# The capacity's cast moved ahead of the last rows, and six gates a step sooner, in a routed expert kernel

## The chip, the cores and the metric

One core of a Trainium2 chip. The metric is the device time of one execution in microseconds (us); three runs of the kernel before are at hand, and one profiled execution.

## The reference

3072 tokens (4 batches of 768) pass through three stages in a row:

```python
for t in range(S):                      # attention: B=4, H=8, S=768, D=40
    y[:, :, t] = einsum('bhd,bhde->bhe', rt, state)
    Sa = einsum('bhde,bhe->bhd', state, at)
    state = state * wt - einsum('bhd,bhe->bhde', Sa, bt) + einsum('bhd,bhe->bhde', vt, kt)
...
logits = x @ w_gate                     # 8 experts, x is 3072 x 320
expert_idx = argmax(logits)             # one expert for each token
gate_w = softmax(logits)[expert_idx]
...
h = maximum(disp[e] @ w1[e], 0)         # 320 -> 1024, up to `capacity` tokens an expert
out[i] = gate_w[i] * (h @ w2[e])        # 1024 -> 320
...
h = x @ w_in                            # 320 -> 2048
out = where(h > 0, h, exp(min(h, 0)) - 1) @ w_out
```

`capacity` is an input (768 here): a token that comes to an expert after its capacity is full gets zeros.

## The kernel before, in words

The program runs in one launch: `attention()` up to about 437 us of the span, then `ffn()`. Every engine works off its instructions in the order in which the program gives them out; nothing is reordered afterwards, so "ahead of" and "behind" in this text mean that order on one engine.

**Attention.** Its steps stand in a table written out by hand (ORDER, from L33 on). Near its end the table has `b22.1 D21 F H22 q23.1`: `b` is `route()`, which picks each token's expert and ends with the sum ACC (L547); `D` scatters a group's rows to the experts' table `disp` in HBM; `F` is `first()` (L597), which makes two index rows on GpSimd (POOL) and issues the loads of the first rows; `q` and what follows (Qs, L487; y, L509; XT, L513; x, L519) is the last group's way through attention. Rows of the first expert that are already in `disp` are loaded from there, transposed (L668), and those of the last two groups of tokens are added by matmuls with a one-hot matrix (L593). The sum stands in the PSUM tiles `pt`.

**Experts.** `experts()` (L1191) makes eight blocks, one for each expert, of 448 slots. `run()` (L1157) goes through their steps. A block has eight steps f = 0 to 7, one for each 128 columns of F. All numbers are split into two parts, a high part (H, XH) and the rest (L, XL), and every product takes the matmuls high by high, low by high and high by low. In step f it gives out, in this order:

- `s1(f)` (L969): eight matmuls of the first layer into a PSUM tile `ph`;
- `s2(f-3)` (L1034 to L1042): eight matmuls of the second layer, into three `po` tiles;
- `act`, here `relu` (L1097), for step f-1: H on ACT (L1099), L on DVE (L1100);
- one piece of the next expert's `load()` (in `rows()`, L1082): it issues the load of X (L1086, on SP), then come two halves of `soft()` (L1068), the softmax that gives the gate g. The first half is a reduction and a subtraction on DVE (L1073, L1074) and an exponential on ACT (L1075); the second half is three DVE instructions (L1077 to L1079). Then four scalings of X by g on ACT (L1093);
- in the last three of the pieces, `prep()` (L944): four transposes on PE into a PSUM tile `pt` (L934), XH on ACT (L953), XL on DVE (L954);
- `extra()`: weight splits, of which the high part is a cast on ACT (L776) and the low part four subtractions on POOL (L781), the fetches of later weights on SP, and pieces of a table conversion on DVE (L859 to L871).

The PSUM tiles of `s1` and the `pt` tiles take turns in four buffers, so a new one waits for the last reader of the tile four before it. A block's result is read out of the `po` tiles while the next block runs (L1047 to L1050). The fifth step of each block (f = 4) gives out the first transposes for the next expert behind its matmuls. Expert 0 has its rows ready in PSUM at the start, unscaled; its gate comes late (`late_gate()`, L1277) and is multiplied in at the end.

Ahead of the first block stand a weight split of four pieces, 16 subtractions on POOL, and `marks()` (L1259), which turns the capacity, an integer of two 32-bit words, to a float: a cast (L1262) and three small instructions (L1263 to L1265), all on DVE. Its users come much later: `gates()` (L1116) and `counts()` (L1372 to L1375).

After the experts come six blocks of the second feed-forward layer, with `elu` in place of `relu`, up to the end. They are not touched.

Of the kernel before, what the change touches and what calls it, by code (L numbers as in the profile page):

```python
# [8 lines left out]
F32 = mybir.dt.float32  # L9
F32R = mybir.dt.float32r  # L10
I32 = mybir.dt.int32
U32 = mybir.dt.uint32
AF = mybir.ActivationFunctionType
ALU = mybir.AluOpType
# [8 lines left out]
SL = 448  # L23
# [52 lines left out]
def attention(tc, nc, e_in, v_tok, d_in, wg, disp, xt, cst, ring, early, early_w, cv, cap, after):  # L76
# [29 lines left out]
    Ws = sh[3][:, 2688:2816].rearrange("p (h t) -> p h t", t=16)  # L106
# [488 lines left out]
    cols, turned = [slice(128 * k, 128 * k + (128, 128, 65)[k]) for k in range(3)], []  # L595

    def first():  # L597
        nc.gpsimd.iota(cst["row"], pattern=[[1, 112]], base=SL, channel_multiplier=0, allow_small_or_imprecise_dtypes=True)
        nc.gpsimd.iota(cst["off"], pattern=[[-112, 4]], base=0, channel_multiplier=0, allow_small_or_imprecise_dtypes=True)
        first_rows(nc, cst, disp)  # L600
# [13 lines left out]
    def warm(n):  # L614
        w = early_w.B[0]
        p = bank("warm")
        for _ in range(n):
            nc.tensor.matmul(p, w[:, 0:128], w[:, 0:512], start=True, stop=True)
    steps = dict(sz=set_z, se=set_e, sa=set_a, sd=set_d, sv=set_v, st=set_t, sr=set_r, ss=set_s, sx=set_x, sw=set_w, sc=set_c, lw=load_w,
                 e=load_e, E=lambda u: load_e(u, eng=nc.scalar), v=load_v, d=load_d, p=pre, a=pre_act, c=scores, m=am_evac, k=kb_tr, l=lm_load, i=solve, o=x_store,  # L620
# [62 lines left out]
def consts(p):  # L683

    c = {}
    c["ident"] = p.tile([128, 128], F32, name="ident")
    c["mask"] = p.tile([128, 64], F32, name="mask")
    for nm in ("ones", "tri"):
        c[nm] = p.tile([128, 128], BF, name=nm)
    c["desc"] = p.tile([128, 8], F32, name="desc")  # L690
    c["ebase"] = p.tile([128, 8], F32, name="ebase")
    c["lg"] = p.tile([128, 24, 9], F32, name="LG")
    c["oh"] = p.tile([128, 2, 8, 12], BF, name="OH")
    c["slot"] = p.tile([128, 24], I32, name="SLOT")
    c["acc"] = p.tile([128, 2, 8], BF, name="ACC")
    c["cap"] = p.tile([128, 2], I32, name="CAP")
    c["x"] = p.tile([128, 2048], F32, name="X0")
    c["xo"] = c["x"][:, 1536:1536 + RW]
    c["row"] = c["x"][:, 1536 + RW:1648 + RW]
    c["off"] = c["x"][:, 1648 + RW:1652 + RW]  # L700
    return c
# [185 lines left out]
def ffn(tc, nc, cst, disp, xt, w1, w2, w32, out, ring, W0, cv, ps, turned):  # L887
# [3 lines left out]
    ap = ctx.enter_context(tc.tile_pool(name="fa", bufs=2))  # L891
# [187 lines left out]
        nc.vector.reciprocal(g, g)  # L1079
        return g  # L1080

    def rows(src, gate=True):  # L1082

        def load(s, now):
            s.X = s.XF[:, 0:4 * RW].rearrange("p (i d) -> p i d", i=4)
            nc.sync.dma_start(out=s.X[0:112], in_=src)  # L1086
            yield
            if not gate:
                return
            yield  # L1090
            g = yield from soft(s)
            for i in range(4):
                nc.scalar.mul(s.X[0:112, i, 0:D], s.X[0:112, i, 0:D], g[:, i:i + 1])  # L1093
            yield
        return load

    def relu(p, H, L):  # L1097
# [18 lines left out]
    def gates():  # L1116

        OH = cst["oh"]
        T = lambda nm, sh, dt=F32: gp.tile(sh, dt, tag="g" + nm, name=nm, bufs=1)
        for nm in ("blk", "tmo", "l1"):  # L1120
            cst[nm] = T(nm, [128, 128], BF)
        set_gates(nc, cst)
        m = T("m", [128, 2, 8, 12])
        nc.vector.memset(m, 1.0)
        nc.vector.memset(m[:, :, :, 0:1], 0.0)
        ic = T("ic", [128, 2, 8, 12], BF)
        nc.vector.tensor_tensor_scan(
            out=ic.rearrange("p b e c -> p (b e c)"), data0=m.rearrange("p b e c -> p (b e c)"),
            data1=OH.rearrange("p b e c -> p (b e c)"), initial=0.0, op0=ALU.mult, op1=ALU.add)
        S = T("S", [128, 2, 8], BF)  # L1130
        nc.vector.tensor_copy(S, ic[:, :, :, 11])
        p = ps.tile([128, 512], F32, tag="ph", name="pg")
        p1 = p[:, 0:192]
        nc.tensor.matmul(p1, cst["tmo"], OH.rearrange("p b e c -> p (b e c)"), start=True, stop=False)
        nc.tensor.matmul(p1, cst["blk"], ic.rearrange("p b e c -> p (b e c)"), start=False, stop=True)
        nc.tensor.matmul(p[:, 192:208], cst["l1"], S.rearrange("p b e -> p (b e)"), start=True, stop=False)
        nc.tensor.matmul(p[:, 200:208], cst["ones"], S[:, 0], start=False, stop=True)
        b = T("b", [128, 2, 8])
        nc.vector.tensor_copy(b.rearrange("p b e -> p (b e)"), p[:, 192:208])
        t = T("t", [128, 2, 8, 12])  # L1140
        nc.vector.tensor_tensor(t, p1.rearrange("p (b e c) -> p b e c", b=2, e=8),
                                b.unsqueeze(3).to_broadcast([128, 2, 8, 12]), op=ALU.add)
        nc.vector.scalar_tensor_tensor(out=t, in0=t, scalar=over["cap"], in1=OH, op0=ALU.is_lt, op1=ALU.mult)
        kp = T("kp", [128, 24])
        nc.vector.tensor_reduce(kp.rearrange("p (c b) -> p b c", b=2), t.rearrange("p b e c -> p b c e"), axis=AX.X, op=ALU.add)
        eb0 = T("eb0", [128, 8])
        nc.vector.tensor_scalar(eb0, cst["ebase"], float(-SL), None, op0=ALU.add)
        nc.vector.tensor_tensor(t, OH, eb0.unsqueeze(1).unsqueeze(3).to_broadcast([128, 2, 8, 12]), op=ALU.mult)
        eb = T("eb", [128, 24])
        nc.vector.tensor_reduce(eb.rearrange("p (c b) -> p b c", b=2), t.rearrange("p b e c -> p b c e"), axis=AX.X, op=ALU.add)  # L1150
        pos, epos = T("pos", [128, 24]), T("epos", [128, 24])
        nc.vector.tensor_tensor(pos, cst["slot"], eb, op=ALU.subtract)
        nc.vector.tensor_scalar(pos, pos, float(-SL), None, op0=ALU.add)
        nc.vector.scalar_tensor_tensor(out=epos, in0=eb, scalar=1.0 / 8, in1=pos, op0=ALU.mult, op1=ALU.add)
        return kp, pos, epos
# [29 lines left out]
    dv = disp.rearrange("(e r i p) d -> e r p i d", e=8, i=4, p=112)  # L1185
# [5 lines left out]
    def experts(r, dyn=False, more=None):  # L1191
# [3 lines left out]
        bl = []  # L1195
        for e in range(8):
# [8 lines left out]
            else:  # L1205
                def store(Y, e=e):
# [1 line left out]
                    nc.sync.dma_start(out=xt[0:256, c].rearrange("(k p) n -> p k n", p=128), in_=Y[:, 0:2])  # L1208
                    nc.sync.dma_start(out=xt[256:D, c], in_=Y[0:64, 2])
                    nc.sync.dma_start(out=xt[D:D + 1, c], in_=Y[64:65, 2])  # L1210
                bl.append(Turned(Ws[e], rows(dv[e, 1], e > 0), relu, store, P=112))
        if dyn:
            for _ in ahead(Ws[0]):
                pass
# [43 lines left out]

    def marks():  # L1259

        cw, cf = cst["cap"], ap.tile([128, 4], F32, name="cf", bufs=1)
        nc.vector.tensor_copy(cf[:, 0:2], cw)  # L1262
        nc.vector.tensor_scalar(cf[:, 2:3], cf[:, 0:1], 0.0, 4294967296.0, op0=ALU.is_lt, op1=ALU.mult)  # L1263
        nc.vector.scalar_tensor_tensor(out=cf[:, 3:4], in0=cf[:, 1:2], scalar=4294967296.0, in1=cf[:, 2:3], op0=ALU.mult, op1=ALU.add)
        nc.vector.tensor_tensor(cf[:, 3:4], cf[:, 3:4], cf[:, 0:1], op=ALU.add)  # L1265
        over["cap"] = cf[:, 3:4]
        one = over["one"] = ap.tile([128, 8], F32, name="one", bufs=1)
        nc.gpsimd.memset(one, 1.0)
        start = over["start"] = ap.tile([128, 6], F32, name="begin", bufs=1)
# [86 lines left out]
    over = {}  # L1356

    def counts():
# [12 lines left out]
        rg = ap.tile([128, 8], F32, name="rg", bufs=1)  # L1371
        nc.vector.tensor_reduce(rn[:, 0:1], cnt, axis=AX.X, op=ALU.max)  # L1372
        nc.vector.tensor_scalar(rn[:, 1:2], rn[:, 0:1], float(SL // 8), None, op0=ALU.add)
        nc.vector.tensor_scalar(rn[:, 2:3], over["cap"], float(SL), None, op0=ALU.min)
        nc.vector.tensor_tensor(rn[:, 2:3], rn[:, 0:1], rn[:, 2:3], op=ALU.is_gt)  # L1375
        yield
        nc.vector.tensor_scalar(rg, cst["ebase"], 1.0 / 8, rn[:, 1:2], op0=ALU.mult, op1=ALU.is_lt)
# [128 lines left out]
```

## Time and profile before

| | us |
|---|---|
| three runs: median (lowest, highest) | 1044.39 (1041.87, 1047.43) |
| the profiled execution, its own time | 1040.54 |
| its span | 1038.7 |
| PE busy | 950.6 (92%) |
| DVE busy | 738.3 (71%) |
| POOL busy | 617.1 (59%) |
| ACT busy | 516.6 (50%) |
| mean granted clock of TensorE | 0.952 of full speed |

All times in the rows are microseconds from the span's start. A row of the timeline has a start, how long a run of like instructions lasts, the engine, the line, what it writes and reads, and how many they are; in brackets how long its engine was idle ahead of it, and what the profile takes for the releaser. Idle time and its releaser are inferred, and where a wait has several causes the last one by the profile is named. PE is TensorE, PEld its weight load, SPq the queue that issues transfers. The profiled execution's 1040.54 us is its span and what lies around it.

### The profile page before, as it was taken

The numbers are of one execution on the slowest core, as the hardware profiler recorded it, in microseconds if no ns is written. First come the engines' busy times: TensorE is split into PE (matmuls) and PEld (weight loads), VectorE is DVE, ScalarE is ACT, GpSimd is POOL, SyncE is SP. The second block draws the span as 40 slices with busy tenths as digits, with TensorE's granted clock in tenths as the row PEclk, the third lists the DMA queues.
The fourth block names the chain that finished last, engine by engine and source line by source line (L and its number), as shares of the span: only waits on it lengthen the run. The fifth ranks groups of instructions, "written<-read, shape, count | busy, mean of one in ns | idle before, by whom it ended". The sixth has DMA issues, their size and how long they took to land.

```text
span 1038.7 us, 25351 instructions
## 1 busy us (share of the span) xinstructions
PE 950.6 (92%) x9994; PEld 860.9 (83%) x9994; DVE 738.3 (71%) x1291; ACT 516.6 (50%) x1013; POOL 617.1 (59%) x929
## 2 busy tenths in 40 slices
PE   4758989989899999789999999999999999999993
PEld 4758878888789888678889888888899888899993
DVE  8846848788675687658778877576766777677760
ACT  3636635666454434245544555565555555554550
POOL 4766979489898833467768787953333333333332
PEclk9967889999899999989999999999999999999997
DMA  6758875666565774646776866501010000100000
GB/s 161 174 159 173 182 162 120 144 139 145 127 120 119 171 195 99 170 141 203 214 236 201 250 186 217 187 23 26 27 27 26 11 28 13 27 26 1 26 2 28
DMA packets 181448, 121.69 MB, mean 117 GB/s; under 512 B 106256, under 2 KB 167336, under 8 KB 179688
## 3 DMA queue, kind: packets, MB, share of 16 engines
q1 hardware_dynamic: 175652, 99.63, 38.0%
q10 hardware_dynamic: 2500, 9.21, 3.4%
q0 software_dynamic: 3168, 11.14, 3.0%
q8 instruction: 81, 1.33, 0.5%
q14 instruction: 47, 0.39, 0.1%
HBM read 86.89 MB, written 33.05 MB: 115 GB/s over the span
## 4 chain that ended last, share of the span: by engine, by line
PE 54%; DVE 17%; DMA 16%; issue 5%; ACT 3%; POOL 3%; SPq 0%; ACTq 0%; DVEq 0%; POOLq 0%
PE ph L969 20%; DMA ring<-in_e_in_dram 5%; PE po L995 5%; PE po L996 5%; PE po L997 5%; DMA w<-E 4%; PE q L482 2%; PE sc L234 2%; DVE L L1100 1%; DVE ring L200 1%; PE x L519 1%; DVE E L860 1%; PE ut L426 1%; PE y L509 1%; DMA dab<-AB 1%
## 5 line engine op out<-in xcount | busy, mean ns | idle before, releaser
L781 POOL TENSOR_TENSOR ring<-ring,ring 128x64 fp32r<-128x64 f32 (+2 forms) x320 | 204.7, 675 | 72.4 <-ACT ring L776 72.4
L1114 POOL TENSOR_TENSOR L<-E,H 128x512 fp32r<-128x512 f32 x66 | 91.6, 1388 | 169.2 <-ACT H L1113 152.5
L969 PE MATMUL ph<-XH,ring 128*128 128x512 f32 (+1 forms) x640 | 169.9, 387 | 0.8 <-ACT XH L953 0.8
L1107 ACT ACTIVATE E<-N 128x512 f32<-128x512 f32 x96 | 60.7, 632 | 152.8 <-DVE N L1106 78.9
L310 POOL TENSOR_TENSOR X<-X,ring 128x60 f32<-128x60 f32 (+19 forms) x170 | 120.4, 708 | 13.3
L969 PEld LDWEIGHTS ph<-XH,ring 128*128 128x128 f32 x640 | 115.7, 190 | 14.9 <-ACT XH L953 1.4
L997 PE MATMUL po<-ring,L 128*128 128x320 f32 x384 | 119.4, 311 | 1.6 <-POOL L L1114 1.6
L995 PE MATMUL po<-ring,H 128*128 128x320 f32 x384 | 119.4, 311 | 0.2 <-ACT H L1113 0.2
L996 PE MATMUL po<-ring,H 128*128 128x320 f32 x384 | 119.2, 310 | 0.0
L969 PE MATMUL ph<-XL,ring 128*128 128x512 f32 (+1 forms) x320 | 97.9, 387 | 7.5 <-DVE XL L954 7.5
L969 PE MATMUL ph<-XS,ring 128*128 128x512 f32 (+1 forms) x320 | 96.9, 384 | 0.0
L1111 DVE SCALAR_TENSOR_TENSOR M<-E,M 128x512 f32<-128x512 f32 x96 | 78.0, 812 | 16.1 <-ACT M L1108 16.1
L1106 DVE TENSOR_SCALAR N<-ph 128x512 f32<-128x512 f32 x96 | 65.8, 685 | 27.7 <-PE ph L969 27.4
L308 POOL TENSOR_TENSOR ring<-X,ring 128x60 f32<-128x60 f32 (+19 forms) x108 | 65.0, 602 | 34.4 <-DMA ring<-dab 26.3
L995 PEld LDWEIGHTS po<-ring,H 128*128 128x128 f32 x384 | 72.8, 190 | 5.2 <-ACT H L1113 0.5
L996 PEld LDWEIGHTS po<-ring,H 128*128 128x128 f32 x384 | 72.7, 189 | 4.0
L969 PEld LDWEIGHTS ph<-XL,ring 128*128 128x128 f32 x320 | 60.7, 190 | 18.4 <-DVE XL L954 8.2
L997 PEld LDWEIGHTS po<-ring,L 128*128 128x128 f32 x384 | 72.7, 189 | 2.1 <-POOL L L1114 2.1
L1112 DVE SCALAR_TENSOR_TENSOR E<-ph,M 128x512 f32<-128x512 f32 x96 | 66.4, 692 | 8.1 <-DVE M L1111 0.5
L969 PEld LDWEIGHTS ph<-XS,ring 128*128 128x128 f32 x320 | 60.3, 189 | 11.2 <-DVE XS L954 0.4
L1100 DVE SCALAR_TENSOR_TENSOR L<-ph,H 128x448 fp32r<-128x448 f32 x64 | 39.4, 616 | 41.3 <-ACT H L1099 41.2
L1113 ACT CAST H<-E 128x512 fp32r<-128x512 f32 x96 | 59.0, 614 | 13.5 <-DVE E L1112 10.4
(261 smaller groups left out, 2176.5 us busy)
## 6 DMA issues: line engine op xcount, KB each, us to landing
ring<-in_w_dram SPq DMA_DIRECT2D x16, 640.0 KB
ring<-in_w_dram SPq DMA_DIRECT2D x32, 256.0 KB
dab<-AB SPq DMA_DIRECT2D x24, 256.0 KB
ring<-in_e_in_dram ACTq DMA_DIRECT2D x18, 321.6 KB
ring<-w SPq DMA_DIRECT2D x4, 1408.0 KB
disp<-ring SPq DMA_DIRECT2D x8, 575.8 KB
S<-in_w_out_dram SPq DMA_DIRECT2D x13, 320.0 KB
ring<-in_w_dram SPq DMA_DIRECT2D x32, 128.0 KB
```

Of the source, the lines that this page charges most:

```text
L308: nc.gpsimd.tensor_tensor(tv, X[:, 0:n, s:s + 1].to_broadcast([128, n, m]), N[:, s:s + 1, s + 1:e].to_broadcast([128, n, m]), op=ALU.mult)
L310: nc.gpsimd.tensor_tensor(X[:, 0:n, s + 1:e], X[:, 0:n, s + 1:e], tv, op=ALU.subtract)
L781: s.nc.gpsimd.tensor_tensor(B[:, to], r[:, q], B[:, q].bitcast(F32), op=ALU.subtract)
L969: nc.tensor.matmul(p, l, r[:, 0:s.T], start=i == 0, stop=i == len(seq) - 1)
L995: nc.tensor.matmul(o, H[:, c], hb, start=f == 0, stop=False)
L996: nc.tensor.matmul(o, H[:, c], lb, start=False, stop=False)
L997: nc.tensor.matmul(o, L[:, c], hb, start=False, stop=f == s.W.nf - 1)
L1106: nc.vector.tensor_scalar(N, p, 0.0, None, op0=ALU.min)
L1107: nc.scalar.activation(out=E, in_=N, func=AF.Exp)
L1111: nc.vector.scalar_tensor_tensor(out=M, in0=E, scalar=1.0, in1=M, op0=ALU.add, op1=ALU.mult)
L1112: nc.vector.scalar_tensor_tensor(out=E, in0=p, scalar=0.0, in1=M, op0=ALU.max, op1=ALU.add)
L1114: eng.tensor_tensor(L, E, H.bitcast(F32), op=ALU.subtract)
```

## The change

Two things. The four instructions that turn the capacity to a float move from `marks()` to `first()`, so from the end of attention's work, ahead of the first block, to the place of `F` in the table; their tile is a constant one. And for the experts 2 to 7 (`e > 1`) `load()` gives out the first half of `soft()` in step 1 in place of step 2, and the second half with the four scalings in step 2 in place of step 3; the transposes stay in step 4.

```diff
     def first():
+        cw, cf = cst["cap"], cst["cf"]
+        nc.vector.tensor_copy(cf[:, 0:2], cw)
+        nc.vector.tensor_scalar(cf[:, 2:3], cf[:, 0:1], 0.0, 4294967296.0, op0=ALU.is_lt, op1=ALU.mult)
+        nc.vector.scalar_tensor_tensor(out=cf[:, 3:4], in0=cf[:, 1:2], scalar=4294967296.0, in1=cf[:, 2:3], op0=ALU.mult, op1=ALU.add)
+        nc.vector.tensor_tensor(cf[:, 3:4], cf[:, 3:4], cf[:, 0:1], op=ALU.add)
         nc.gpsimd.iota(cst["row"], pattern=[[1, 112]], base=SL, channel_multiplier=0, allow_small_or_imprecise_dtypes=True)
...
-    def rows(src, gate=True):
+    def rows(src, gate=True, soon=False):
 
         def load(s, now):
             s.X = s.XF[:, 0:4 * RW].rearrange("p (i d) -> p i d", i=4)
...
             if not gate:
                 return
-            yield
+            if not soon:
+                yield
             g = yield from soft(s)
             for i in range(4):
                 nc.scalar.mul(s.X[0:112, i, 0:D], s.X[0:112, i, 0:D], g[:, i:i + 1])
             yield
+            if soon:
+                yield
         return load
...
-                bl.append(Turned(Ws[e], rows(dv[e, 1], e > 0), relu, store, P=112))
+                bl.append(Turned(Ws[e], rows(dv[e, 1], e > 0, e > 1), relu, store, P=112))
...
     def marks():
 
-        cw, cf = cst["cap"], ap.tile([128, 4], F32, name="cf", bufs=1)
-        nc.vector.tensor_copy(cf[:, 0:2], cw)
...
-        over["cap"] = cf[:, 3:4]
         one = over["one"] = ap.tile([128, 8], F32, name="one", bufs=1)
```

The readers of the capacity name the new tile. The changed kernel's lines stand some 5 to 9 further down (L954 becomes L959, L1100 becomes L1108).

What moves on DVE, at the end of attention and the start of the first block. Before, the four instructions stand between the last one-hot matrix and XL:

```order
L547 TENSOR_TENSOR ACC<-ACC,roh 128x8
L487 TENSOR_TENSOR Qs<-q,mask 128x512 x2
...
L588 TENSOR_TENSOR hot<-X_73,pos 128x448
L1262 CAST cf<-CAP 128x2
L1263 TENSOR_SCALAR cf<-cf 128x1
L1264 SCALAR_TENSOR_TENSOR cf<-cf 128x1
L1265 TENSOR_TENSOR cf<-cf 128x1
L954 TENSOR_TENSOR XL<-pt,XH 128x448 x2
```

In the changed kernel they stand behind ACC and ahead of Qs:

```order
L547 TENSOR_TENSOR ACC<-ACC,roh 128x8
L599 CAST CF<-CAP 128x2
L600 TENSOR_SCALAR CF<-CF 128x1
L601 SCALAR_TENSOR_TENSOR CF<-CF 128x1
L602 TENSOR_TENSOR CF<-CF 128x1
L487 TENSOR_TENSOR Qs<-q,mask 128x512 x2
...
L588 TENSOR_TENSOR hot<-X_74,pos 128x448
L959 TENSOR_TENSOR XL<-pt,XH 128x448 x2
```

XL is now the first instruction behind the one-hot matrix.

The gate on DVE, in the block that brings expert 3 (L859 to L866 are pieces of the table conversion, L1048 and L1050 read out the block before). The three rows of L1100 are the L of steps 0, 1 and 2. Before:

```order
L1100 SCALAR_TENSOR_TENSOR L<-ph,H 128x448
L859 TENSOR_SCALAR N<-S_7095 128x320
...
L1048 COPY Y<-po 128x448
L1050 TENSOR_TENSOR Y<-po,half 64x448
L1100 SCALAR_TENSOR_TENSOR L<-ph,H 128x448
L1073 TENSOR_REDUCE g<-X_73 112x4
L1074 TENSOR_TENSOR x<-X_73,g 112x32
L1100 SCALAR_TENSOR_TENSOR L<-ph,H 128x448
L1077 TENSOR_REDUCE g<-x 112x4
L1078 TENSOR_SCALAR g<-g 112x4
L1079 RECIPROCAL g<-g 112x4
```

In the changed kernel:

```order
L1108 SCALAR_TENSOR_TENSOR L<-ph,H 128x448
L1078 TENSOR_REDUCE g<-X_74 112x4
L1079 TENSOR_TENSOR x<-X_74,g 112x32
L864 TENSOR_SCALAR N<-S_7095 128x320
...
L1053 COPY Y<-po 128x448
L1055 TENSOR_TENSOR Y<-po,half 64x448
L1108 SCALAR_TENSOR_TENSOR L<-ph,H 128x448
L1082 TENSOR_REDUCE g<-x 112x4
L1083 TENSOR_SCALAR g<-g 112x4
L1084 RECIPROCAL g<-g 112x4
L1108 SCALAR_TENSOR_TENSOR L<-ph,H 128x448 x2
```

The first half went from behind the L of step 1, called L(1) below, to behind L(0), the second half from behind L(2) to behind L(1).

The same place on ACT. Before, the four scalings (L1093) stand behind H of step 2:

```order
L1047 COPY Y<-po 128x448
L1049 COPY half<-po 64x448
L1099 ACTIVATE H<-ph 128x448
L1075 ACTIVATE x<-x 112x32
L776 CAST ring_7221<-ring_7047 128x704
L1099 ACTIVATE H<-ph 128x448
L1093 ACTIVATE X_73<-X_73,g 112x320 x4
L776 CAST ring_7221<-ring_7047 128x704
L1099 ACTIVATE H<-ph 128x448
L953 CAST XH<-pt 128x448
```

In the changed kernel:

```order
L1080 ACTIVATE x<-x 112x32
L781 CAST ring_7221<-ring_7047 128x704
L1052 COPY Y<-po 128x448
L1054 COPY half<-po 64x448
L1107 ACTIVATE H<-ph 128x448
L1099 ACTIVATE X_74<-X_74,g 112x320 x4
L781 CAST ring_7221<-ring_7047 128x704
L1107 ACTIVATE H<-ph 128x448
L781 CAST ring_7221<-ring_7047 128x704
L1107 ACTIVATE H<-ph 128x448
```

The scalings now stand behind H of step 1 and ahead of H of step 2, H(2).

## Rows read from the trace of the kernel before

**Rows 1.** The page: busy time of the engines, share of the span.

```profile
PE 950.6 (92%) x9994; PEld 860.9 (83%) x9994; DVE 738.3 (71%) x1291; ACT 516.6 (50%) x1013; POOL 617.1 (59%) x929
```

**Rows 2.** Waits from 436 to 680 us: total us, times, longest.

```profile
ACT X L1093 <- DVE g L1079: 8.7, 6, 1.5
...
PEld pt L934 <- ACT X L1093: 8.0, 22, 0.9
```

**Rows 3.** Timeline of the expert stage's start, POOL, DVE and PE.

```profile
436.72 8.28 POOL L781 TENSOR_TENSOR ring<-ring,ring 128x64 fp32r<-128x64 f32 x16
...
436.85 8.24 DVE L1262 CAST cf<-CAP 128x2 f32<-128x2 int32 x1 [2.60 <-DMA ring<-in_w_dram]
445.12 0.15 DVE L1263 TENSOR_SCALAR cf<-cf 128x1 f32<-128x1 f32 x1
...
445.58 1.15 DVE L954 TENSOR_TENSOR XL<-pt,XH 128x448 fp32r<-128x448 f32 x2
...
437.41 1.30 PE L969 MATMUL ph<-XH,ring 128*128 128x448 f32 x4 [0.75 <-ACT XH L953]
446.25 1.27 PE L969 MATMUL ph<-XL,ring 128*128 128x448 f32 x2 [7.54 <-DVE XL L954]
...
455.76 0.96 PE L969 MATMUL ph<-XH,ring 128*128 128x448 f32 x4
```

**Rows 4.** Stretches: length, busy PE, PEld, DVE, ACT, POOL, clock, DMA share, GB/s.

```profile
440.00:443.00 3.00, 0.00 (x0) 0.00 (x0) 3.00 (x1) 0.00 (x0) 3.00 (x7) 0.50 0.71 180
...
446.00:450.00 4.00, 3.75 (x9) 2.89 (x10) 1.97 (x4) 1.07 (x2) 0.00 (x0) 0.50 0.86 215
```

**Rows 5.** Timeline from 406 us, a DVE copy beside POOL.

```profile
406.22 1.73 DVE L527 COPY XO<-LG 128x9 f32<-128x9 f32 x1
...
406.40 2.11 POOL L781 TENSOR_TENSOR ring<-ring,ring 128x64 fp32r<-128x64 f32 x4
```

**Rows 6.** Timeline of the end of attention, DVE and POOL.

```profile
426.11 1.28 DVE L487 TENSOR_TENSOR Qs<-q,mask 128x512 f32<-128x512 f32 x2
...
431.63 0.89 POOL L584 TENSOR_TENSOR hot<-X,hot 128x321 fp32r<-128x321 f32 x1 [5.67 <-ACT hot L583]
```

**Rows 7.** Timeline of the first block: DVE, ACT and PE.

```profile
452.14 0.18 DVE L1073 TENSOR_REDUCE g<-X 112x4 f32<-112x32 f32 x1
...
456.03 1.93 ACT L1093 ACTIVATE X<-X,g 112x320 f32<-112x320 f32 x4 [1.38 <-DVE rn L1372]
...
458.96 0.55 PE L934 MATMUL pt<-ident,X 112*128 112x112 f32 x4
```

**Rows 8.** Timeline of PE in the block that brings expert 3.

```profile
511.45 0.96 PE L969 MATMUL ph<-XH,ring 128*128 128x448 f32 x4
...
515.29 1.68 PE L934 MATMUL pt<-ident,X 112*128 112x112 f32 x4 [0.48 <-ACT X L1093]
516.74 1.06 PE L969 MATMUL ph<-XH,ring 128*128 128x448 f32 x4
```

**Rows 9.** Timeline of DVE there.

```profile
510.93 0.60 DVE L1100 SCALAR_TENSOR_TENSOR L<-ph,H 128x448 fp32r<-128x448 f32 x1
511.46 0.17 DVE L1073 TENSOR_REDUCE g<-X 112x4 f32<-112x32 f32 x1
...
513.26 0.62 DVE L1100 SCALAR_TENSOR_TENSOR L<-ph,H 128x448 fp32r<-128x448 f32 x1 [1.41 <-ACT H L1099]
...
517.74 0.62 DVE L1100 SCALAR_TENSOR_TENSOR L<-ph,H 128x448 fp32r<-128x448 f32 x1 [3.10 <-ACT H L1099]
```

**Rows 10.** Timeline of ACT there.

```profile
514.68 1.92 ACT L1093 ACTIVATE X<-X,g 112x320 f32<-112x320 f32 x4 [1.45 <-DVE g L1079]
```

**Rows 11.** DMA busy tenths, 471 to 479 us in 40 slices; timeline of SP and DVE.

```profile
DMA  6689979798998899999999977320001286999998
...
471.25 0.38 SPq L1086 DMA_DIRECT2D X<-disp  x1
...
476.44 0.61 DVE L1100 SCALAR_TENSOR_TENSOR L<-ph,H 128x448 fp32r<-128x448 f32 x1
```

More of the change, by code (lines that the diff above doesn't have):

```diff
@@ L695, in consts @@
     c["acc"] = p.tile([128, 2, 8], BF, name="ACC")
-    c["cap"] = p.tile([128, 2], I32, name="CAP")
+    c["cap"], c["cf"] = p.tile([128, 2], I32, name="CAP"), p.tile([128, 4], F32, name="CF")
     c["x"] = p.tile([128, 2048], F32, name="X0")
@@ L1142, in gates @@
                                 b.unsqueeze(3).to_broadcast([128, 2, 8, 12]), op=ALU.add)
-        nc.vector.scalar_tensor_tensor(out=t, in0=t, scalar=over["cap"], in1=OH, op0=ALU.is_lt, op1=ALU.mult)
+        nc.vector.scalar_tensor_tensor(out=t, in0=t, scalar=cst["cf"][:, 3:4], in1=OH, op0=ALU.is_lt, op1=ALU.mult)
         kp = T("kp", [128, 24])
@@ L1259, in marks @@
     def marks():
-        cw, cf = cst["cap"], ap.tile([128, 4], F32, name="cf", bufs=1)
-        nc.vector.tensor_copy(cf[:, 0:2], cw)
-        nc.vector.tensor_scalar(cf[:, 2:3], cf[:, 0:1], 0.0, 4294967296.0, op0=ALU.is_lt, op1=ALU.mult)
-        nc.vector.scalar_tensor_tensor(out=cf[:, 3:4], in0=cf[:, 1:2], scalar=4294967296.0, in1=cf[:, 2:3], op0=ALU.mult, op1=ALU.add)
-        nc.vector.tensor_tensor(cf[:, 3:4], cf[:, 3:4], cf[:, 0:1], op=ALU.add)
-        over["cap"] = cf[:, 3:4]
         one = over["one"] = ap.tile([128, 8], F32, name="one", bufs=1)
@@ L1373, in counts @@
         nc.vector.tensor_scalar(rn[:, 1:2], rn[:, 0:1], float(SL // 8), None, op0=ALU.add)
-        nc.vector.tensor_scalar(rn[:, 2:3], over["cap"], float(SL), None, op0=ALU.min)
+        nc.vector.tensor_scalar(rn[:, 2:3], cst["cf"][:, 3:4], float(SL), None, op0=ALU.min)
         nc.vector.tensor_tensor(rn[:, 2:3], rn[:, 0:1], rn[:, 2:3], op=ALU.is_gt)
```

## The prediction

> **What bounds the kernel now.** I read the page first, then the waits of the expert stage, then the timeline and the stretches around the two places that the change touches. On the page TensorE (PE) is busy for 92% of the span [rows 1], so only stretches in which PE stands still, or runs at its lower clock, can give time. Two such stretches lie where this change works.
>
> The first is the start of the expert stage. PE begins the first expert's first step at 437.41 and then has nothing from 438.71 until 446.25, an idle of 7.54 us put down to XL, which VectorE (DVE) makes [rows 3]. DVE was in one instruction for all that time: the cast of capacity, 128x2 numbers, took 8.24 us, from 436.85 to 445.09. GpSimd (POOL) ran 16 subtractions of the weight split back to back from 436.72 to 445.00 [rows 3], so the cast ended 0.09 us after the last of them. XL followed at 445.58. [...]
>
> The second comes once in each of the experts 2 to 7, at the fifth step of the block before. The transposes of the next expert's rows wait for their scaling on ScalarE (ACT): 8.0 us in 22 waits, and the scaling waits for the gate g, 8.7 us in 6 waits [rows 2]. In the block that brings expert 3, the fifth step starts at 511.45; its 16 matmuls take 3.20 us, so the transposes could start at 514.65. They started at 515.29, lasted 1.68 us, and the sixth step came at 516.74 [rows 8].
>
> **The cast.** Is POOL really what the cast waited for? A second case says so: a copy of 128x9 numbers took 1.73 us while POOL ran 4 such subtractions, 2.11 us in all [rows 5]. It ended at 407.95 (406.22 + 1.73), not after the first of them, which would be about 406.93 (2.11 / 4 = 0.53 each): it missed at least two chances. The cast missed fifteen. So a DVE instruction of this kind can be kept out as long as POOL's subtractions follow each other without a gap. [...]
>
> The change puts the cast and its three small successors behind the ACC sum and ahead of Qs. POOL is idle there: its instruction at 431.63 has 5.67 us of idle before it, so from 425.96 on, and Qs starts at 426.11 [rows 6]. At the old place the three successors took from 445.12 to 445.58, 0.15 each [rows 3]; with no POOL beside it the cast of two numbers should be near that, and I take 0.67 us for the four. They delay Qs, and the attention's tail to the first expert hangs on it, so all 0.67 is on the path. Bounds: 0 if the tail has slack, 1.5 if the cast meets a stray POOL instruction.
>
> At the expert start, XL then follows XH. PE's first matmuls come at 437.41 + 0.67 = 438.08. XL can start about then as well; it takes 1.15 for its two pieces and about 0.6 for XS, then two more matmuls: the first step ends at about 440.3. Three more first-layer steps and one second-layer step, each 8 matmuls or 1.6 us at full clock (half of the 3.20 above), bring the fifth step to 446.7. It started at 455.76 [rows 3]: 9.0 us sooner. That holds the 7.54 of idle, and what the half clock cost. If the clock falls all the same, some 1 us of it is lost again.
>
> Not all of this lasts. Expert 1's gate is not moved, and its rows are loaded by a transfer issued at 439.80, that waits for the attention's last scatter and so moves with the tail (to 440.5), not with PE. From its first reduction at 452.14 to the end of the four scalings at 457.96 there are 5.8 us, and the transposes came at 458.96 [rows 7], so 1.0 us to spare. After the change the reduction can follow the second L at about 443.2 at the earliest, or the landing; a load of the same kind, issued at 471.25, was down by 476.4, since from there the DMA engines show nothing [rows 11], so 445.6 is the latest. The scalings would then end between 449.0 and 451.4, where PE wants to transpose at 458.96 - 9.0 = 449.95. The loss is 0 to 1.5; I take 0.7. **First part: -8.3 us** (already with the 0.67), between -9.0 and -4.5, the latter if this block's DVE work meets POOL's next run as well.
>
> **The gate, six times.** The first half of softmax (reduction 0.17, subtraction about 0.19) goes ahead of the table conversions and of the evictions on DVE; the second half follows L(1) in place of L(2). On ACT the exponential moves up a step, and the four scalings now stand ahead of a weight split and of H(2). POOL's and SP's orders, PE's too, stay; no transfer is added or moved. What hides the moved instructions is that they are the same ones in the same queues.
>
> Now the scaling is a step sooner: before, L(2) ended at 513.88 and the scalings began at 514.68 [rows 9, 10]; now g follows L(1), which ended at 511.53 [rows 9] and comes some 0.36 later, at 511.89, since the first half stands ahead of it. The scalings begin at about 512.7 and end by 514.6, and the transposes find them done. But H(2) now waits behind the four scalings, and L(2) waits for H(2). L(2) is the last reader of the PSUM buffer that the sixth step writes (four buffers go round, and the transposes take one of them). The price of that queue stands in the rows, one place later: from L(2)'s end, 513.88, to L(3)'s, 517.74 + 0.62 = 518.36 [rows 9], with the gate, the four scalings (1.92 [rows 10]), a weight split and H between, 4.48 us. So now L(2) ends at 511.89 + 4.48 = 516.37, and the sixth step, which came at 516.74, comes at about 516.4. The gain is some 0.35 to 0.4 and not the 1.5 or so that the wait had. **Second part: 6 x 0.4 = -2.4 us.** Bounds: -8.0, the whole wait [rows 2], if L(2) isn't what ends last; +2, if the earlier subtraction, with both inputs in SBUF, stands behind a POOL instruction in each block and the evictions behind it (0.3 each).
>
> **Sum.** -8.3 - 2.4 = -10.7 us: the profiled execution of 1040.54 us would become 1029.8. The three runs have their median at 1044.39, 3.85 above it; against that median the forecast is **1033.7 us**. About 0.5%, 5.2 us, is what a measurement of this kernel can tell from no change.
>
> **Rivals.**
> 1. The PSUM wait doesn't bind, and the transposes' wait goes whole: -8.3 - 7 = -15.3, 1029.1 us. For it: the waits name the scalings alone. Against: the 4.48 us of rows 9. Chance 0.12.
> 2. The collision with POOL is met elsewhere. In the first block the subtraction of expert 1's gate, and the cast of the tokens' offsets behind it, now come around 444 to 446, while POOL's run lasts to 445.0, and its next one is only an ACT cast away. If one of them is kept out for about 4 us, L(2) and the sixth step are late by that: -6.7, 1037.7 us. Chance 0.13.
> 3. The change doesn't do what it says: the 8.24 us belong to the place. [...] Then only +0.67 - 2.4 is left: 1042.7 us. For it: the wait ahead of the cast is put down to a transfer, and XL comes next on the engine. Against: the copy of rows 5, and that the end agrees with POOL's to 0.09 us. Chance 0.11.
> 4. Slower: the gate's first half now stands ahead of five or more DVE instructions, L(1) among them. If the next expert's rows have not landed, DVE stands there, and L(1), L(2) and the sixth step are late by the wait w, less 0.4. Where would that decide? 6 x (w - 0.4) must exceed 8.3 + 5.2, so w above 2.65 us in each block; with 3 us the time is 1044.39 - 8.3 + 15.6 = 1051.7. Against: the load issued at 471.25 was down by 476.4, and its reduction would now come at 477.05, behind the L at 476.44 [rows 11], 0.6 us later; in the block of expert 3 the margin is wider. It is the tightest margin that I found. Chance 0.04.
>
> **How the numbers follow.** The forecast has 0.60. Forecast, rival 1 and most of rival 2 are faster by over 0.5% (1039.2 us): 0.60 + 0.12 + 0.11 = 0.83. Rival 3 and the rest of rival 2 are within it: 0.13. Rival 4 is slower: 0.04. The range goes from 1028.0, rival 1 with the better end of the first part, to 1039.0, past rival 2; rivals 3 and 4 are left out, 15 in 100.
>
> **What would show it.** Right: the cast at about 426.3 in under 0.3 us; XL at about 438, with POOL's run still going on beside it; PE without an idle of more than 1 us from 438 to 447, and a granted clock near 1.00 from 440 to 450; the fifth step near 446.7. In six blocks the first transposes last 0.6 to 1.0 us and not 1.4 to 1.7, and a new wait stands in the list, of PE or its weight load at the sixth step for L on DVE, about 1 us each. Wrong: a DVE instruction of several us beside a POOL run in the first block (rival 2), XL still at about 445 (rival 3), DVE waiting for X's transfer at the reduction (rival 4), or the sixth step without a wait (rival 1).

## The result, and the profile after

The changed kernel took 1035.22 us in the median of 17 runs, the kernel before 1044.39 in 17. The ratio is 0.9894, 95% interval 0.9866 to 0.9921: 11 us faster, between 8 and 14. The medians alone lie 9.2 us apart. The forecast was 10.7 us (1033.7). The profiled execution took 1029.08 us, its span is 1027.2.

The timeline of the changed kernel shows the four moved instructions, and the start of the first block, in answer to [rows 3, 6, 7]:

```profile
427.11 0.16 DVE L547 TENSOR_TENSOR ACC<-ACC,roh 128x8 bf16<-128x8 bf16 x1
427.19 0.16 DVE L599 CAST CF<-CAP 128x2 f32<-128x2 int32 x1
427.39 0.15 DVE L600 TENSOR_SCALAR CF<-CF 128x1 f32<-128x1 f32 x1
...
427.84 1.28 DVE L487 TENSOR_TENSOR Qs<-q,mask 128x512 f32<-128x512 f32 x2
...
437.58 8.42 POOL L786 TENSOR_TENSOR ring<-ring,ring 128x64 fp32r<-128x64 f32 x16
...
439.13 1.16 DVE L959 TENSOR_TENSOR XL<-pt,XH 128x448 fp32r<-128x448 f32 x2 [3.13 <-ACT XH L958]
...
439.15 1.31 PE L974 MATMUL ph<-XH,ring 128*128 128x448 f32 x4 [0.75 <-ACT XH L958]
440.30 0.57 PE L974 MATMUL ph<-XL,ring 128*128 128x448 f32 x2
...
446.13 0.19 DVE L1078 TENSOR_REDUCE g<-X 112x4 f32<-112x32 f32 x1 [1.60 <-DMA X<-disp]
...
448.15 0.97 PE L974 MATMUL ph<-XH,ring 128*128 128x448 f32 x4
...
451.41 0.93 PE L939 MATMUL pt<-ident,X 112*128 112x112 f32 x4
```

The cast takes 0.16 us; Qs starts at 427.84, 0.65 us behind the cast's start at 427.19, where it would stand without the four. XL starts beside POOL's run, 6.9 us ahead of its end, and takes what it took without POOL (1.16). PE's second row follows the first without a gap. The same stretches as in [rows 4] show the clock:

```profile
440.00:443.00 3.00, 2.88 (x15) 2.26 (x13) 1.53 (x3) 1.07 (x2) 3.00 (x6) 1.00 0.18 53
446.00:450.00 4.00, 4.00 (x22) 3.62 (x21) 2.05 (x10) 2.07 (x4) 2.88 (x14) 1.00 0.73 188
```

PE is busy and its granted clock is 1.00 in both, where it was 0.50 in both before. The waits from 428 to 680 us answer to [rows 2]:

```profile
ACT X L1099 <- DVE g L1084: 11.4, 6, 2.6
...
PEld ph L974 <- DVE L L1108: 3.1, 6, 0.8
...
DVE g L1078 <- DMA X<-disp: 2.1, 2, 1.6
PE ph L974 <- DVE L L1108: 1.8, 4, 0.6
...
PEld pt L939 <- ACT X L1099: 0.3, 1, 0.3
```

The transposes' wait for the scalings has gone from 8.0 us to 0.3, and PE's wait for L stands in its place, six times, as the prediction had it, though with 0.5 us each (3.1 in all) where it had about 1. In the block that brings expert 3, against [rows 8 to 10]:

```profile
504.78 0.98 PE L974 MATMUL ph<-XH,ring 128*128 128x448 f32 x4
508.05 0.55 PE L939 MATMUL pt<-ident,X 112*128 112x112 f32 x4
508.77 1.08 PE L974 MATMUL ph<-XH,ring 128*128 128x448 f32 x4 [0.17 <-DVE L L1108]
...
503.87 0.61 DVE L1108 SCALAR_TENSOR_TENSOR L<-ph,H 128x448 fp32r<-128x448 f32 x1
...
508.09 0.62 DVE L1108 SCALAR_TENSOR_TENSOR L<-ph,H 128x448 fp32r<-128x448 f32 x1 [3.10 <-ACT H L1107]
...
505.02 1.92 ACT L1099 ACTIVATE X<-X,g 112x320 f32<-112x320 f32 x4 [1.33 <-DVE g L1084]
```

The transposes last 0.55 us, and the sixth step starts 0.06 us after L(2) ends (508.71). L(2) ends 4.23 us after L(1) (504.48): the queue of gate, scalings, split and H that the prediction priced at 4.48.

Where did the 11.5 us between the two spans come from? The starts of each block's first matmul in the timeline give this:

| piece of the span, us | before | after | difference |
|---|---|---|---|
| start to the first block | 437.41 | 439.15 | +1.74 |
| first block | 32.40 | 23.61 | -8.79 |
| blocks 2 to 7 | 170.06 | 168.65 | -1.41 |
| block 8, not touched | 25.60 | 26.07 | +0.47 |
| second feed-forward stage, to PE's end | 358.11 | 355.35 | -2.76 |
| the rest | 15.1 | 14.4 | -0.7 |

Of the +1.74, 0.65 are the moved instructions; ACC itself was 1.08 later already, and the change moves no instruction ahead of it. Two rows are a surprise: a block that wasn't touched is longer by 0.47, and a stage that wasn't touched is shorter by 2.76.

### The profile page after: what moved, and what is told of

Its sections match the earlier page's. It is cut to its first block, busy times and chain, and to the rows that moved or that the text cites. A ratio compares the mean times of both kernels' runs of the same rounds, so it can differ in the third digit from the quotient of the medians.

```text
span 1027.2 us, 25350 instructions
## 1 busy us (share of the span) xinstructions
PE 946.0 (92%) x9994; PEld 855.5 (83%) x9994; DVE 726.8 (71%) x1291; ACT 516.2 (50%) x1013; POOL 613.1 (60%) x929
## 3 DMA queue, kind: packets, MB, share of 16 engines
q8 instruction: 81, 1.33, 0.5%
## 4 chain that ended last, share of the span: by engine, by line
PE 52%; DVE 14%; DMA 12%; POOL 9%; issue 5%; SPq 3%; ACT 3%; ACTq 0%; POOLq 0%; DVEq 0%
PE ph L974 19%; PE po L1000 5%; PE po L1002 5%; PE po L1001 5%; POOL ring L308 3%; POOL X L310 3%; DMA ring<-in_e_in_dram 3%; PE q L482 3%; DMA w<-E 3%; DMA dab<-AB 2%; PE y L509 2%; PE ut L426 1%; PE y L496 1%; DVE L L1108 1%; PE st L451 1%
## 5 line engine op out<-in xcount | busy, mean ns | idle before, releaser
L310 POOL TENSOR_TENSOR X<-X,ring 128x60 f32<-128x60 f32 (+19 forms) x170 | 115.2, 677 | 13.3
L308 POOL TENSOR_TENSOR ring<-X,ring 128x60 f32<-128x60 f32 (+19 forms) x108 | 70.1, 649 | 36.6 <-DMA ring<-dab 28.6
L1119 DVE SCALAR_TENSOR_TENSOR M<-E,M 128x512 f32<-128x512 f32 x96 | 75.5, 786 | 14.8 <-ACT M L1116 14.6
L1108 DVE SCALAR_TENSOR_TENSOR L<-ph,H 128x448 fp32r<-128x448 f32 x64 | 39.4, 616 | 37.6 <-ACT H L1107 37.5
```

What stands on the lines that cost most here:

```text
L308: nc.gpsimd.tensor_tensor(tv, X[:, 0:n, s:s + 1].to_broadcast([128, n, m]), N[:, s:s + 1, s + 1:e].to_broadcast([128, n, m]), op=ALU.mult)
L310: nc.gpsimd.tensor_tensor(X[:, 0:n, s + 1:e], X[:, 0:n, s + 1:e], tv, op=ALU.subtract)
L1119: nc.vector.scalar_tensor_tensor(out=M, in0=E, scalar=1.0, in1=M, op0=ALU.add, op1=ALU.mult)
```

## The experiments

The 14 profiles (the changed kernel has two) reach the first block anywhere from 428.8 to 443.1 us, the changed kernel itself at 439.2 and 430.5: attention's length varies that much from execution to execution. In r2 and r4, which reach it first, attention's mean granted clock is 0.94 and PE is busy for 368 us of it; in the other twelve the clock is 0.90 to 0.92 and PE is busy for 376 to 381. Why the clock differs there stays open. So I read the stages from the traces, and the ratios only as a frame. In the tables below "experts" runs from the first block's first matmul to the end of block 8.

**One part alone.** Three kernels and the changed one on one chip.

r1_cast_only is the changed kernel with

```diff
-                bl.append(Turned(Ws[e], rows(dv[e, 1], e > 0, e > 1), relu, store, P=112))
+                bl.append(Turned(Ws[e], rows(dv[e, 1], e > 0), relu, store, P=112))
```

and r2_gate_only is the kernel before with `rows()` of the changed one and

```diff
-                bl.append(Turned(Ws[e], rows(dv[e, 1], e > 0), relu, store, P=112))
+                bl.append(Turned(Ws[e], rows(dv[e, 1], e > 0, e > 1), relu, store, P=112))
```

> The changed kernel with the gates of experts 2 to 7 where they were: only the capacity's four instructions are moved. Theory (the cast was kept out by POOL's 16 subtractions): -8.3 us against before, XL at the start of the first block within 1 us of PE's first matmul, a granted clock of 1.00 at the start of the stage. The six blocks' fifth steps as before, 4.4 to 5.3 us. Rival (the 8 us belong to the place, not to the cast): about +0.7 us, XL still 8 us behind.

> Kernel before with the six gates a step sooner; the capacity's cast stays ahead of XL. Theory (the sixth step now waits for L of step 2, whose H stands behind the four scalings): -2.4 us against before, up to -4 where the conversions on DVE meet less of POOL; the six fifth steps 3.8 to 4.4 us, with a wait of PE or its weight load for L. Rival (the transposes' wait goes whole): -7 us, fifth steps 3.65. The cast again about 8 us.

> The changed kernel itself on the chip of the other three, for comparison: -11 us against before, fifth steps 3.8 to 4.4 us.

| | ratio to before, interval | first block | blocks 2 to 7 | experts |
|---|---|---|---|---|
| before (profile) | | 32.40 | 170.06 | 228.05 |
| r1_cast_only | 0.9885 (0.9837 to 0.9934) | 23.23 | 173.00 | 222.29 |
| r2_gate_only | 0.9921 (0.9884 to 0.9959) | 33.37 | 168.66 | 227.63 |
| r4_changed | 0.9818 (0.9776 to 0.9860) | 23.38 | 171.99 | 221.43 |

The cast alone brings the whole gain of the first block, 9.2 us less the 0.65 in the tail, and leaves the transposes' wait where it was (8.1 us in 22 waits). The gate alone leaves the cast at 8.17 us and takes 1.4 us from the six blocks. Its ratio says more, at least 4 us; its experts are shorter by 0.4 only, and its profile reached the first block at 428.8. What shortened its profiled run lies in attention, which this edit doesn't touch; for the other runs there is no trace, and I can't say what it was. r4 is the changed kernel again: 19 us faster than before on this chip, 11 in the first measurement; its profile reached the first block at 430.5. By the ratios the parts add up (12.0 and 8.2 us against 19.0 together), by the experts' length they give 5.8, 0.4 and 6.6, so half or more of what the ratios show on this chip lies outside the experts and is not explained.

**Was it POOL's run, and is it the cast's kind of instruction?** Two edits to the kernel before. r5_half_run leaves two pieces of the split ahead of the block and gives out the others in its first step:

```diff
-        go(second, 5)
+        go(second, 2)
...
+            if b == 0 and f == 0:
+                go(second, 5)
```

r6_reduce_for_cast has another instruction at the same place; the three small ones go to `counts()`:

```diff
-        nc.vector.tensor_copy(cf[:, 0:2], cw)
+        nc.vector.tensor_reduce(cf[:, 0:2], cw.unsqueeze(2), axis=AX.X, op=ALU.max)
```

> Kernel before, but of the weight split's four pieces only two stand ahead of the first block; the other two follow within its first step. POOL's run at the cast is 8 subtractions in place of 16, the cast and its place are the same. Theory (the cast waits until POOL's run ends): the cast lasts about 4.2 us in place of 8.2, and the kernel is about 4 us faster. Rival (something of the place, not POOL): the cast's end and the time stay, within 1 us. [...]

> Kernel before, but at the same place the cast is done by a reduction over an axis of length 1 (same values), and the three small instructions behind it go to a later place in the first block. Reductions of one input ran unstretched beside POOL (0.17 us). Theory (POOL keeps out the cast's kind of instruction, not the place): the reduction takes 0.2 us beside POOL's 16 subtractions, XL follows at once, and the time falls by 7 to 9 us. Rival (the place holds DVE): no change, the reduction ends at 445 as well. The three small ones may be kept out by POOL up to 445, which would take back 1 to 2 us.

The timeline of r5_half_run, POOL and DVE:

```profile
438.87 4.17 POOL L781 TENSOR_TENSOR ring<-ring,ring 128x64 fp32r<-128x64 f32 x8
...
438.99 4.22 DVE L1264 CAST cf<-CAP 128x2 f32<-128x2 int32 x1 [2.59 <-DMA ring<-in_w_dram]
```

The timeline of r6_reduce_for_cast, POOL and DVE:

```profile
437.55 8.41 POOL L781 TENSOR_TENSOR ring<-ring,ring 128x64 fp32r<-128x64 f32 x16
...
437.96 0.15 DVE L1262 TENSOR_REDUCE cf<-CAP 128x2 f32<-128x2 int32 x1 [2.59 <-POOL ring L781]
438.50 1.16 DVE L954 TENSOR_TENSOR XL<-pt,XH 128x448 fp32r<-128x448 f32 x2 [0.39 <-ACT XH L953]
```

Half the run, half the wait: the cast took 4.22 us beside 8 subtractions and 8.24 beside 16. And a reduction at the very place of the cast goes through beside POOL in 0.15 us. The first block is 28.75 us long in r5 and 23.64 in r6, against 32.40; the ratios are 0.9964 (0.9935 to 0.9994) and 0.9894 (0.9855 to 0.9933). So the place has no part in it.

Not every DVE instruction was kept out like this. A later run of POOL in the changed kernel is as long and has no gap either; the timeline, POOL and DVE:

```profile
452.71 9.24 POOL L786 TENSOR_TENSOR ring<-ring,ring 128x64 fp32r<-128x64 f32 x16 [0.83 <-ACT ring L781]
...
457.35 0.56 DVE L1079 TENSOR_TENSOR x<-lgx,g 112x32 f32<-112x32 f32 x1
...
458.18 0.82 DVE L865 SCALAR_TENSOR_TENSOR E<-S,N 128x320 int32<-128x320 int32 x1
```

Beside it the subtraction of a gate took 0.56 us and the pieces of the table conversion 0.31 to 0.82 us, and no DVE instruction beside that run took longer. The copy of [rows 5], too, was done at 407.95, while POOL's run went on to 408.51. What lets one instruction in and keeps the cast out was not tried.

**What limits the fifth steps now?** r12_scalings_alone is the changed kernel with the scalings given out behind H(2):

```diff
             g = yield from soft(s)
+            if soon:
+                yield
             for i in range(4):
                 nc.scalar.mul(s.X[0:112, i, 0:D], s.X[0:112, i, 0:D], g[:, i:i + 1])
             yield
-            if soon:
-                yield
         return load
```

r3_scalings_later has that and, in `soft()`, the yield of these six gates ahead of the exponential in place of behind it:

```diff
+        if wait:
+            yield
         nc.scalar.activation(out=x, in_=x, func=AF.Exp)
-        yield
+        if not wait:
+            yield
```

> The changed kernel, but on ACT the exponential stands behind the evictions of the block before, and the four scalings behind H of step 2; DVE's order is that of the changed kernel. If the wait for L of step 2 is what limits the sixth step, H and L of step 2 now run in the time in which ACT waited for the gate, the scalings begin no later, and the fifth steps come down to about 3.65 us: 2 to 3 us faster than the changed kernel, -13 to -14 against before. If the scalings' end is what limits, nothing or a little slower than the changed kernel, since they end up to 0.6 us later.

> The changed kernel with the four scalings behind H of step 2, the exponential left ahead of the evictions: half of r3_scalings_later. If the fifth steps are long through L of step 2 alone, they come down to 3.6 us here as well, while fourth steps of 3.6 to 4.1 us still occur in some blocks, where PE waits for a result tile that ACT has not read out, since ACT stands at the exponential. If the fifth steps stay near 4 us, the exponential's place takes part in them.

The timeline of r12_scalings_alone in the block that brings expert 3, PE, ACT and DVE:

```profile
507.69 0.98 PE L974 MATMUL ph<-XH,ring 128*128 128x448 f32 x4
510.96 0.55 PE L939 MATMUL pt<-ident,X 112*128 112x112 f32 x4
511.27 1.05 PE L974 MATMUL ph<-XH,ring 128*128 128x448 f32 x4
...
506.30 0.55 ACT L1107 ACTIVATE H<-ph 128x448 fp32r<-128x448 f32 x1
507.08 1.93 ACT L1101 ACTIVATE X<-X,g 112x320 f32<-112x320 f32 x4 [0.23 <-DVE g L1084]
...
506.96 0.59 DVE L1108 SCALAR_TENSOR_TENSOR L<-ph,H 128x448 fp32r<-128x448 f32 x1
```

H(2) now runs while ACT would wait for the gate (0.23 us of idle are left of 1.33), L(2) ends at 507.55, and the sixth step waits for nothing. All six fifth steps take 3.57 or 3.58 us, where the changed kernel's take 3.82 to 4.40. Blocks 2 to 7 take 164.42 us, against 168.65. So the wait for L(2) was the whole excess of the fifth steps. (r12 was run once, so only its trace counts; r3's fifth steps are the same, 3.57 and 3.58.)

Leaving the second block aside, single fourth steps are long as well, up to 4.27 us. In the changed kernel it is that of block 5, with 3.96 us; the timeline there, ACT and PE:

```profile
557.54 0.23 ACT L1080 ACTIVATE x<-x 112x32 f32<-112x32 f32 x1 [6.93 <-DVE x L1079]
...
558.35 0.53 ACT L1052 COPY Y<-po 128x448 f32<-128x448 f32 x1
...
558.92 0.47 PE L1040 MATMUL po<-H,ring 128*128 128x448 f32 x1 [0.20 <-ACT Y L1052]
```

ACT stood for 6.93 us ahead of the exponential, which the change put in front of the readouts, and PE waited for the tile that ACT read out 0.81 us behind it. The same stands in long fourth steps of r2 (4.13 and 4.10 us), r4 (3.96), r7 (3.92) and r10 (4.23). In r3, r9 and r11, which have the exponential behind the readouts, no fourth step waits for ACT; in r12, which has it ahead, none did either, in its one profile. r1 and r6, whose gates weren't moved, have one long fourth step each (4.08 and 4.27), but of another cause: ACT had read out its tile in time, and PE waited for the one that DVE reads out (0.56 and 0.79 us of idle). PE waited for DVE's tile in one fourth step each of r2, r4 and r11, too (3.84, 3.71 and 3.71).

r3 was 0.9818 (0.9779 to 0.9858), the same as r4 beside it, though its blocks 2 to 7 are 5.7 us shorter (166.28 against 171.99); r4's profile reached the first block 9.0 us earlier than r3's (430.5 against 439.5), which would cover that.

In its second block r3 lost 1.9 us, as r4 did. The timeline of r4_changed there:

```profile
464.84 0.19 DVE L1078 TENSOR_REDUCE g<-X 112x4 f32<-112x32 f32 x1 [3.22 <-DMA X<-disp]
...
468.15 0.47 PE L1040 MATMUL po<-H,ring 128*128 128x448 f32 x1 [1.60 <-DVE Y L1058]
```

DVE waits 3.22 us for expert 2's rows, the result tiles are read out late, and PE stands. That is the fourth rival, in one block of six, and not with the same size in every execution: in the first profile of the changed kernel expert 2's rows cost DVE 0.53 us (of the 2.1 in the list above, 1.60 are expert 1's).

**Why is an untouched block longer?** Its 128 matmuls are the same, in the same order. Block 8 as one stretch, columns as in [rows 4], from the changed kernel, r8_only_32_bytes, r7_tile_64_bytes and r10_ring_against_data:

```profile
631.41:657.48 26.07, 26.07 (x130) 23.61 (x128) 17.68 (x28) 15.03 (x27) 26.07 (x43) 1.00 0.57 186
```

```profile
645.99:671.59 25.60, 25.60 (x129) 23.61 (x128) 18.25 (x28) 15.37 (x27) 25.60 (x42) 1.00 0.55 181
```

```profile
631.12:657.18 26.06, 26.06 (x129) 23.60 (x128) 17.93 (x28) 15.03 (x27) 26.06 (x43) 1.00 0.57 184
```

```profile
636.40:662.00 25.60, 25.60 (x129) 23.59 (x128) 17.76 (x28) 15.01 (x27) 25.60 (x42) 1.00 0.57 185
```

The clock is 1.00 in all, PE is busy without a break, and yet there are two lengths: 25.60, 200 ns for a matmul, and 26.07, 203.7 ns. Of the kernels told of so far, those with the capacity's tile moved had the longer one, r2, r5 and r6 the shorter one. The moved tile shifts what the program places behind it.

In r7_tile_64_bytes, against the changed kernel:

```diff
-    c["cap"], c["cf"] = p.tile([128, 2], I32, name="CAP"), p.tile([128, 4], F32, name="CF")
+    c["cap"], c["cf"] = p.tile([128, 2], I32, name="CAP"), p.tile([128, 16], F32, name="CF")
```

In r8_only_32_bytes, against the kernel before, an unused tile:

```diff
+    c["gap32"] = p.tile([128, 4], F32, name="GAP32")
```

In r10_ring_against_data, against the changed kernel, an unused tile at the old one's place:

```diff
+        ap.tile([128, 4], F32, name="spare", bufs=1)
```

> The changed kernel, but its new constant tile has 16 numbers in place of 4, so that the tiles behind it, the weights' ring among them, lie 64 bytes and not 32 further on than before. In the four kernels with the 4-number tile the matmuls of an expert's undisturbed step are 196 to 212 ns apart, 3.25 to 3.27 us a step; in the four without it 200 ns and 3.20 us. If the ring's place is the cause: 3.20 us a step again, the experts some 3 us shorter (0.055 us in each of some 60 steps), the second feed-forward stage about 1 us longer (355.0 to 356.2). If it is something else of the change: 3.25 us.

> Kernel before with one thing added: an unused constant tile of 16 bytes behind the capacity's, which moves the ring by 32 bytes. If the ring's place sets the matmuls' distance: 3.25 to 3.27 us for an undisturbed step in place of 3.20, the cast still about 8 us, and the time +2 us or so, not to be told from no change. If not: 3.20.

> The changed kernel with an unused tile of 16 bytes where the old capacity tile stood, behind the ring and ahead of XH, H and L. In all kernels so far with 3.20 us a step the ring's addresses and XH's differ by 32 modulo 64; in all with 3.25 they agree modulo 64, wherever both lie. Moving only one of them took the difference away; this puts it back. If that is the cause: 200 ns between matmuls and 3.20 us a step, the experts some 3 us shorter than with 3.25, second feed-forward stage 1 us longer. If not: 3.25.

My first guess, the place of the weights' ring, fell twice: 64 bytes didn't bring the 25.60 back, 32 bytes alone didn't take it away. What fits all kernels, by the places that the program gives its tiles (no trace shows them), is the distance between the ring (the weights that PE loads) and the tiles XH, XL, H and L (the data that stream through), modulo 64 bytes: 32 in the kernel before, in r2, r5, r6 and r8; 0 in the changed kernel, r1, r3, r4, r7, r9 and r12. r10 puts 32 back by one unused tile, and has 25.60. So the change carries a cost of its own that no instruction shows: about 0.06 us in an undisturbed step (0.47 in eight), by estimate some 3 us over the experts' 64 steps. r7 and r10 differ by 2.4 us over the experts (221.29 and 218.92), but their waits differ as well. In the second feed-forward stage it goes the other way with the same distance: it takes 355.35 us in the changed kernel, r3, r4 and r7, and 356.50 in r6 and 356.34 in the kernel of r11 below. Why distance matters was not tried. The other 1.7 us of that stage go with a dip of the granted clock near its end, in some executions. Stretches there of the kernel before and of the changed kernel:

```profile
1016.00:1021.00 5.00, 4.66 (x21) 4.66 (x22) 0.57 (x2) 0.43 (x1) 1.88 (x4) 0.66 0.09 33
```

```profile
1005.40:1010.40 5.00, 4.14 (x25) 3.75 (x26) 0.57 (x2) 0.76 (x2) 2.76 (x5) 1.00 0.09 33
```

r1, r2, r5, r8, r9, r10 and r12 have the dip too, with and without the moved instructions, so it is not the change's.

**Together.** r9 and r11 take r3's order of ACT and leave expert 2's gate at its old place; r9 with r7's tile, r11 with r10's.

```diff
-                bl.append(Turned(Ws[e], rows(dv[e, 1], e > 0, e > 1), relu, store, P=112))
+                bl.append(Turned(Ws[e], rows(dv[e, 1], e > 0, e > 2), relu, store, P=112))
```

> The order of ACT of r3_scalings_later (exponential behind the evictions, scalings behind H of step 2), the gate of expert 2 left at its old place, since its rows land late, and the 64-byte tile. Undisturbed steps 3.20 us; the fifth steps of the five blocks from the third on 3.5 to 3.6 us; no wait of DVE for X in the second block, whose fifth step is 4.4 to 4.8. From the start of the first block to the end of the experts about 213 to 215 us, against 228 before and 218 to 221 for the changed kernel; the time -14 to -16 us against before.

> r9_combined with the 4-number tile and the unused tile of r10_ring_against_data, so with the ring's and XH's addresses 32 apart modulo 64. If the distance is the cause: 3.20 us a step, 3.52 in place of 3.58 for the fifth steps, from the first block's start to the end of the experts 212 us in place of 214.9; the time -14 to -16 us against before.

| | ratio to before, interval | undisturbed step | blocks 2 to 7 | experts |
|---|---|---|---|---|
| r7_tile_64_bytes | 0.9880 (0.9839 to 0.9922) | 3.25 | 171.07 | 221.29 |
| r8_only_32_bytes | 0.9977 (0.9955 to 1.0000) | 3.20 | 170.76 | 229.24 |
| r9_combined | 0.9846 (0.9808 to 0.9884) | 3.25 | 165.57 | 214.86 |
| r10_ring_against_data | 0.9900 (0.9850 to 0.9950) | 3.20 | 170.18 | 218.92 |
| r11_combined_again | 0.9813 (0.9766 to 0.9859) | 3.20 | 164.47 | 214.24 |

r9's steps stayed at 3.25, against its expectation, and its experts are in the range by the fifth steps alone (3.58 in five blocks). r11 has 3.20 and 3.52 to 3.53, as expected, but its first block's fifth step took 4.69 us, and three other steps were 0.2 to 0.5 us longer than in r9, so its experts are 214.24 us long and not 212. Both beat the kernel before; r11, 1025.26 us in the median and 19.5 us below before by its ratio, has the lowest ratio of all, but can't be told from the changed kernel on record: r4's ratio is 0.9818, with a median of 1024.65.

## Why the prediction was right

**The cast.** The mechanism and its size held. The first block gained 8.79 us in the changed kernel and 9.2 in r1, the tail lost 0.65 (forecast 0.67); the forecast's net was -8.3, the trace gives -8.1 and -8.5. XL, the clock (1.00 where it was 0.50) and the missing idle are where they were forecast, and r5 and r6 show the cause: POOL's run (4.22 us beside 8 subtractions), and the cast in place of a reduction (0.15 us beside 16). The third rival fell with r6. The second did not come: no DVE instruction in the changed kernel's first block took more than 0.82 us. It was priced with a stay of about 4 us for a subtraction; the one beside POOL's run of 452.71 took 0.56. Expert 1's load set the loss in the first block, as the prediction had it: DVE waited 1.60 us for it, and the fifth step took 3.95 us where r1's took 3.57, so 0.4 against the 0.7 taken; over all profiles with the cast out of the way that step took 3.57 to 4.69 us, so a loss of up to 1.1 us, within the 0 to 1.5 given. The fifth step came 9.00 us after the block's first matmul (448.15 - 439.15), where the forecast had 8.6.

**The gate.** The new wait, its place and the queue behind it held; r12, which takes the queue away, shows it to be the whole of the fifth steps' excess. The size, -2.4, is right in part by luck: at equal matmul distance the six blocks gained 4.35 (changed kernel against r1), 1.9 (r7 against r1), 1.0 (r4 against r1) and 1.4 us (r2 against before), and lost 0.1 in r10 against before: 1.7 in the mean, and two terms where the prediction had one. The six fifth steps together took 28.8 to 29.8 us in before, r5, r6 and r8, and 24.8 and 26.0 in r2 and r10, all at one distance: they gained about 4 us. The six fourth steps together took 19.2 to 20.3 us in the first four and 21.7 and 22.1 in the other two: they lost about 2.4 (1.7 of r10's loss through expert 2's late rows), and for what the exponential does there the prediction had no term. It noted that the exponential moves up a step on ACT, and did not ask what stands behind it there.

Two more things spread the size. L(1) came earlier in some blocks, beside shorter conversions: in the block of expert 3 L(1) ended 3.60 us after L(0) had in the changed kernel, though two instructions more lie between, and 4.09 before; the four conversions ahead of it took 0.32 to 0.52 us each where they had taken 0.49 to 0.82. POOL's run had ended at 500.00 there, before the first of them (501.12); before, it went on beside them, from 507.36 to 509.24. And expert 2's rows were late.

**The step that was off** is the fourth rival's margin. I took it from a load that was down 5.2 us after its issue, before [rows 11], and called it the tightest. In r4 the load issued at 455.82 held DVE until 464.84, 9 us later. In the five other profiles with a short first block and expert 2's gate early (changed kernel, r3, r7, r10, r12) DVE waited 0.53 to 2.97 us and had the rows 6.3 to 8.8 us after the issue; in r2, whose first block is long, it went on 5.8 us after the issue without a wait. My estimate from these times, which no run tests, is that a first block that is 9 us shorter puts the same transfers closer together, with the load of X behind them; why the load took 6.3 us in one execution of the changed kernel and 9.0 in another is not shown. I moved the load and its use forward alike and did not ask what the shorter stage does to the transfers. The rival met the second block, and others with a wait of 1.5 us at most (r11), so it cost some 2 us and not the sign.

**What no part of the prediction had:** the 0.06 us per step from the tile's place, by estimate some 3 us lost, and about 1 us won back in the second stage. That the total came within 0.4 us of the ratio's 11.1 is luck by that much: the clock's dip and attention's own length move the time as far.

## What to carry to other kernels

A small DVE instruction ahead of a critical one is worth a look at what POOL runs beside it: a small cast was kept out for the whole of a back-to-back run (8.24 us), while a reduction (0.15 us) and the two pieces of XL (1.16 us) went through beside such a run, and table conversions beside one took 0.82 us at most; so look at the trace and don't infer it from the engine. When work is moved a step sooner, look at what now queues behind it, on every engine that it touches: giving out the four scalings one instruction later kept the early gate and took the new wait away (fifth steps of 3.57 or 3.58 us where they were 3.82 to 4.40), and an exponential that waited 6.93 us for its input held up the readouts behind it, so that PE waited 0.20 us. A new tile moves what the program places behind it; if an untouched stage changes its pace (here 203.7 ns for a matmul in place of 200), compare the distance of the operands' places before looking for a cause in the instructions.

## What was not expected of the hardware

- The distance of weights and data in SBUF modulo 64 bytes, by the places in the program, goes with the distance of matmuls of 448 columns in all 14 profiles: 200 ns at 32, 203.4 to 203.7 at 0, at the same granted clock (1.00 in the four stretches above), and r10 put it back as expected (3.20 us a step); the second stage is shorter at the other (355.4 us at 0, 356.3 and 356.5 at 32).
- A DVE cast was kept out through sixteen POOL instructions in a row (8.24 us for 128x2 numbers), while conversions beside another run of sixteen (9.24 us) took 0.82 us at most.
- Attention's length varied by 14 us between profiles, with the same work in it; the two shortest have the higher granted clock (0.94 against 0.90 to 0.92). The cause stays open, and so does what the gate alone won beyond its 0.4 us in the experts.
